# Hash attention with feed-forward: loads of batch 0 regrouped, head halves kept in the first four steps, and the whole order remade

## The chip, the cores and the metric

The kernel runs on one core of a Trainium2 chip. The metric is device time in microseconds (us), lower is better. Each kernel was executed several times; one execution was also recorded by the profiler. The profile gives a span (first to last instruction, 1.7 us less than the device time in the two profiled executions of before) and the mean clock that the throttle granted to TensorE, where 1 is full speed and the records show only full and half. An execution is called slow here when it is more than 1.5% above the fastest of the same kernel, else fast. Means below are of fast runs unless the text says otherwise.

The engines are named as in the profile: PE is TensorE, PEld its weight loads, DVE is VectorE, ACT is ScalarE, POOL is GpSimd, SP is SyncE. SPq, ACTq and POOL `DMA_DIRECT2D` lines are issues of transfers.

## The reference

Inputs q, k, v have shape (4, 8, 768, 64), `proj` is (64, 6), the feed-forward weights are 512x2048 and 2048x512.

```python
q_bits = (einsum('bhsd,dk->bhsk', q, proj) > 0)     # 6 hash bits per row
k_bits = (einsum('bhsd,dk->bhsk', k, proj) > 0)
mask   = (bucket of q == bucket of k)               # all six bits agree
scores = where(mask, q @ k.T / 8, -1e9)
x      = softmax(scores) @ v                        # heads joined to (4, 768, 512)
xn     = (x - mean) / sqrt(var + 1e-6) * g_ln
out    = x + relu(xn @ w_ch1) @ w_ch2
```

## The kernel before

The whole schedule is one string of words, `operation.engine.arguments`. A loop reads the string once and emits the instructions. Each engine then executes its own words strictly in that order, and waits where the data of a word is not there yet.

```python
with tc.manual_schedule():
    for word in ORDER.split():
        name, eng, *args = word.split(".")
        OPS[name](ENGINES[eng], *map(int, args))     # v DVE, a ACT, p POOL, s SP, t PE
```

A step s (0 to 71) stands for 256 query rows (u = s//6), a group of four heads (g) and a block of 256 keys (kp = s%3). The words that matter here:

```python
def lx(eng, g, t, kp):                 # batch 0: load a third of q (t=0) or k (t=1), 256 KB
    src = qk_view(t, 0, g).rearrange("p (c kp x) -> p kp c x", c=CC, kp=3)
    dst = Xt(0, g, t).rearrange("p (c kp x) -> p kp c x", c=CC, kp=3)
    eng.dma_start(out=dst[:, kp], in_=src[:, kp])

def tn(eng, g, t, kp):                 # transpose that third, on DVE
    for j in range(2):
        turn(tp(g, t, kp), Xt(0, g, t), j, 2 * kp, 2)

def ca(eng, g, t, kp):                 # cast it to bf16, on any of three engines
    cast(eng, t, qk(t, 0, g)[:, :, 256 * kp : 256 * kp + 256], tp(g, t, kp))

# ha: hash matmul on PE.  bi: its sign as "bits", on DVE, into G.
# lv: a v load of 32 partitions.  cv/su/sp/sc: cast of v, and its sum over the rows.

def lw1(eng, n):                       # a quarter of the first weights, cast by the DMA
    nc.gpsimd.dma_start(out=w1_sb[:, :, 512*n : 512*n+512], in_=w1ap[:, :, 512*n : 512*n+512])

def heads(h):                          # h = 0, 1: a half of the heads; h = 2: all four
    return slice(0, 4) if h == 2 else slice(2 * h, 2 * h + 2)

def S_(eng, s, h):                     # scores on PE: the bits G (6 rows), then q and k (32 rows)
    for kk in range(2):
        for rep in range(3):
            for i in range(4)[heads(h)]:
                ...                    # one matmul, 256 columns
def E_(eng, s, h):                     # exponential on ACT
    nc.scalar.activation(E(s)[:, heads(h)], sc(s, h), AF.Exp, scale=EXP_SCALE, bias=bias_sb)
# A: attention times v on PE.  na nb nc ce: division, layer norm on DVE.
# F R D: feed-forward 1, relu, feed-forward 2.  Z: residual.  O: output store.
# LX tu CA hm bt mo: loads, transposes, casts and hashes of batches 1 to 3.
```

There are three buffers for E, one score PSUM tile per half of the heads, and four buffers for X.

The softmax here doesn't subtract the row's maximum and nothing guards it: scores larger than these inputs give would overflow.

## Time and profile before

| | before |
|---|---|
| device time, median of 3 | 319.82 us (319.4 to 319.95) |
| profiled execution (a slow one) | 326.67 us, span 325.0, clock 0.957 |
| PE busy | 310.7 us (96%) |
| half-clock stretch | 24.3 to 51.6 us |

The first fence has lines of the profile page: busy time of PE, then PE's busy tenths and granted clock in 40 slices of 8.1 us.

```profile
PE 310.7 (96%) x4320; PEld 211.8 (65%) x4320; DVE 182.9 (56%) x356; ACT 182.0 (56%) x198; POOL 91.5 (28%) x102
...
PE   6869999999989999999999999999999999999993
...
PEclk9995558999999999999999999999999999999999
```

From the fourth slice on TensorE is nearly always busy, so time is lost only where the clock digit drops or where TensorE stands. Most of both lies in the first 60 us. The table by stretches shows it; the columns are the stretch, its length, then busy time (and count) of PE, PEld, DVE, ACT and POOL, granted clock, DMA share and GB/s.

```profile
20.00:25.00 5.00, 2.45 (x35) 1.69 (x31) 2.71 (x8) 2.12 (x2) 2.38 (x5) 0.93 1.12 235
25.00:40.00 15.00, 15.00 (x150) 9.89 (x151) 8.80 (x18) 6.58 (x6) 10.79 (x14) 0.50 0.91 201
40.00:50.00 10.00, 9.85 (x115) 7.00 (x108) 6.68 (x16) 6.65 (x7) 2.30 (x3) 0.50 1.24 205
```

TensorE works half of 20 to 25 us, then runs at half speed to the end of these lines. What stood before the gap is in the timeline of DVE; the bracket gives the idle time before the instruction and what ended it.

```profile
22.03 2.07 DVE L244 STREAM_TRANSPOSE tp<-X 128x256 f32<-128x256 f32 x6 [3.43 <-DMA X<-in_q_dram]
```

DVE stood 3.43 us for a piece of q that is used only some steps later, and held up all of its later words. The chain of work that ended last (start, duration, what) has the same transfer, and later two loads of v for batch 1:

```profile
4.92 5.60 DMA X<-in_k_dram
10.53 11.40 DMA X<-in_q_dram
...
72.04 6.15 DMA vn<-in_v_dram
...
80.26 2.12 DMA vn<-in_v_dram
```

This profile fell on a slow execution.

### The profile page before, as it was taken

Reading aid. Unit: us, or ns where it says so; the run is one execution under the profiler, and the core shown is the slowest. Engines: PE = TensorE matmul, PEld = TensorE weight load, DVE = VectorE, ACT = ScalarE, POOL = GpSimd, SP = SyncE. Lnnn points to the kernel's source line nnn. Section 1 sums busy time; section 2 is a strip of 40 time slices with the busy share of each in tenths; the row PEclk is TensorE's granted clock in tenths of the full one; section 3 lists DMA queues with packets and bytes.
Section 4 is the critical chain, followed back from the end, with each engine's and each line's share of the span. In section 5 each row is a group of like instructions: output and inputs, shape, how many; then the busy total and the mean of one; then the engine's idle time right before and its main releaser. Section 6 shows DMA issues by size and latency. Waiting matters only on the chain.

```text
span 325.0 us, 9793 instructions
## 1 busy us (share of the span) xinstructions
PE 310.7 (96%) x4320; PEld 211.8 (65%) x4320; DVE 182.9 (56%) x356; ACT 182.0 (56%) x198; POOL 91.5 (28%) x102
## 2 busy tenths in 40 slices
PE   6869999999989999999999999999999999999993
PEld 6555767766656767657677667666667666766651
DVE  4547475716645958765825628914635546446441
ACT  3553476666456676646756656764776675771000
POOL 2065822603470054474220056700300100001000
PEclk9995558999999999999999999999999999999999
DMA  7999799146117981463154140111220400402122
GB/s 198 216 219 275 130 205 162 23 133 165 51 38 272 302 189 57 144 173 119 22 146 86 32 117 0 39 25 23 53 53 2 114 20 2 99 2 48 50 67 65
DMA packets 33354, 33.59 MB, mean 103 GB/s; under 512 B 15648, under 2 KB 29984, under 8 KB 33312
## 3 DMA queue, kind: packets, MB, share of 16 engines
q1 hardware_dynamic: 29008, 28.77, 34.9%
q0 software_dynamic: 4224, 4.19, 8.0%
q8 instruction: 34, 0.56, 0.8%
q14 instruction: 8, 0.07, 0.1%
q10 hardware_dynamic: 80, 0.00, 0.0%
HBM read 27.53 MB, written 6.29 MB: 104 GB/s over the span
## 4 chain that ended last, share of the span: by engine, by line
PE 78%; DMA 8%; DVE 6%; SPq 4%; POOL 2%; issue 1%; ACT 0%; DVEq 0%; ACTq 0%
PE f L477 24%; PE f L492 23%; PE sc L405 17%; PE acc L420 11%; DMA X<-in_q_dram 4%; DMA vn<-in_v_dram 3%; SPq L382 2%; PE hp L370 2%; DVE xc L450 2%; DMA X<-in_k_dram 2%; PE hf L306 2%; SPq L292 1%; DVE st L446 1%; DVE x L442 1%; DVE y L433 1%
## 5 line engine op out<-in xcount | busy, mean ns | idle before, releaser
L411 ACT ACTIVATE E<-sc,bias_sb 128x1024 bf16<-128x1024 f32 x144 | 153.7, 1111 | 82.2 <-PE sc L405 80.3
L477 PE MATMUL f<-xnT,w_sb 128*128 128x256 bf16 x768 | 99.2, 273 | 0.5 <-DVE hb L487 0.5
L492 PE MATMUL f<-w_sb,hb 128*128 128x512 bf16 x384 | 93.6, 379 | 0.0
L477 PEld LDWEIGHTS <-w_sb 128*128 128x128 bf16 x768 | 70.8, 98 | 23.4 <-issue 9.9
L487 DVE TENSOR_SCALAR hb<-f 128x512 bf16<-128x512 f32 x53 | 36.6, 691 | 63.8 <-PE f L477 63.5
L405 PE MATMUL sc<-qb,kb 32*128 32x256 bf16 x1152 | 62.9, 281 | 0.0
L492 PEld LDWEIGHTS <-hb 128*128 128x128 bf16 x384 | 35.6, 98 | 35.4 <-issue 3.8
L405 PE MATMUL sc<-G 6*128 6x256 bf16 x576 | 48.6, 285 | 0.4 <-ACT E L411 0.2
L420 PEld LDWEIGHTS <-E 128*128 128x128 bf16 x1152 | 43.3, 100 | 8.0 <-issue 5.1
L420 PE MATMUL acc<-vaug,E 128*128 128x65 bf16 x1152 | 46.9, 198 | 0.2 <-POOL vaug L328 0.2
L405 PEld LDWEIGHTS <-kb 32*128 32x128 bf16 x1152 | 35.5, 98 | 3.2
L485 ACT ACTIVATE hb<-f 128x512 bf16<-128x512 f32 x43 | 25.6, 596 | 20.6 <-PE f L477 20.5
L455 POOL TENSOR_SCALAR rs<-mv 128x2 f32<-128x2 f32 x12 | 8.5, 710 | 98.1 <-DVE mv L449 97.8
L497 DVE SCALAR_TENSOR_TENSOR res<-f,rs,x 128x512 f32<-128x512 f32 x24 | 17.9, 745 | 28.3 <-PE f L492 21.6
L405 PEld LDWEIGHTS <-G 6*128 6x128 bf16 x576 | 17.3, 94 | 22.4 <-issue 19.5
L244 DVE STREAM_TRANSPOSE T<-X 128x384 f32<-128x384 f32 x48 | 24.9, 553 | 3.6 <-DMA X<-in_k_dram 3.4
L336 POOL TENSOR_TENSOR t<-vn 128x768 f32<-128x768 f32 x8 | 15.2, 1905 | 34.6 <-DMA vn<-in_v_dram 20.2
L328 POOL CAST vaug<-vn 128x768 bf16<-128x768 f32 x16 | 13.9, 889 | 39.0 <-DMA vn<-in_v_dram 30.3
L433 DVE SCALAR_TENSOR_TENSOR y<-vsB,acc 128x520 f32<-128x520 f32 x24 | 16.5, 689 | 9.0 <-PE acc L420 8.7
L450 DVE SCALAR_TENSOR_TENSOR xc<-x,mv,gB 128x512 bf16<-128x512 f32 x24 | 19.9, 829 | 0.9
L306 PE MATMUL hf<-tp,pfull 128*128 128x256 f32 x48 | 15.1, 447 | 5.2 <-DVE tp L244 4.2
L442 DVE TENSOR_TENSOR x<-y,rc 128x512 f32<-128x512 f32 x24 | 18.4, 767 | 0.8
(49 smaller groups left out, 153.1 us busy)
## 6 DMA issues: line engine op xcount, KB each, us to landing
vn<-in_v_dram SPq DMA_DIRECT2D x32, 192.0 KB
out_dram<-res SPq DMA_DIRECT2D x44, 128.0 KB
X<-in_q_dram SPq DMA_DIRECT2D x6, 768.0 KB
X<-in_k_dram SPq DMA_DIRECT2D x6, 768.0 KB
w_sb<-in_moe_w_ch_dram POOLq DMA_DIRECT2D x8, 512.0 KB, 11.1
X<-in_k_dram SPq DMA_DIRECT2D x6, 256.0 KB
X<-in_q_dram SPq DMA_DIRECT2D x6, 256.0 KB
G<-B SPq DMA_DIRECT2D x96, 4.5 KB
```

The costliest lines, as they stand in the source:

```text
L244: nc.vector.transpose(d[:, j], s[:, j, kj0 : kj0 + n])
L306: nc.tensor.matmul(hf(g, t, kp)[:, :256], pfull[:, j], tp(g, t, kp)[:, j], start=(j == 0), stop=(j == 1))
L405: nc.tensor.matmul(sc(s, i // 2)[:, i % 2, 256 * kk : 256 * kk + 256], lh, rh, start=(rep == 0), stop=(rep == 2), skip_group_check=True,)
L411: nc.scalar.activation(E(s)[:, heads(h)], sc(s, h), AF.Exp, scale=EXP_SCALE, bias=bias_sb)
L420: nc.tensor.matmul(acc[:, qt, (D + 1) * i : (D + 1) * (i + 1)], E(s)[:, i, 256 * kk + P * qt : 256 * kk + P * qt + P], vaug(u // 3)[:, 4 * ...
L433: nc.vector.scalar_tensor_tensor(yt(u, g), vs, EPS_ROW, made[f"acc{u}{g}"][:, :, :A], op0=AOP.mult, op1=AOP.add,)
L442: nc.vector.tensor_tensor(xo, a[:, :, :, 0:D], rc.to_broadcast([P, 2, 4, D]), op=AOP.mult)
L450: nc.vector.scalar_tensor_tensor(xc(u)[:, t], xt(u)[:, t], mv(u)[:, t, 0:1], gB, op0=AOP.subtract, op1=AOP.mult,)
L477: nc.tensor.matmul(f1[:, n].rearrange("p (t x) -> p t x", t=2), w1_sb[:, dt, P * nt : P * nt + P], xnT(u)[:, :, dt], start=(dt == 0), stop ...
L485: nc.scalar.activation(hb(u)[:, 2 * p : 2 * p + 2], f1, AF.Relu)
L487: eng.tensor_scalar_max(hb(u)[:, 2 * p : 2 * p + 2], f1, 0.0)
L492: nc.tensor.matmul(f2, hb(u)[:, nt, P * t : P * t + P], w2_sb[:, nt], start=(nt == 0), stop=(nt == NNT - 1),)
```

## The change

The intent is to load batch 0 with fewer, larger transfers on two hardware queues, to have the weights early, to avoid the cost of head halves as soon as the start is over, and to lay the order out anew around that.

```diff
-    def lx(eng, g, t, kp):
-        src = qk_view(t, 0, g).rearrange("p (c kp x) -> p kp c x", c=CC, kp=3)
-        dst = Xt(0, g, t).rearrange("p (c kp x) -> p kp c x", c=CC, kp=3)
-        eng.dma_start(out=dst[:, kp], in_=src[:, kp])
+    def lx(eng, g, t, kp0, kp1):
+        src = qk_view(t, 0, g).rearrange("p (c kp x) -> p c kp x", c=CC, kp=3)
+        dst = Xt(0, g, t).rearrange("p (c kp x) -> p c kp x", c=CC, kp=3)
+        eng.dma_start(out=dst[:, :, kp0:kp1], in_=src[:, :, kp0:kp1])
```

The rest is the order string. "..." marks cuts:

```diff
  loads of batch 0, in the order of their queues
- SP:   lx.s.0.1.1 lx.s.0.0.0 lx.s.0.1.0 lx.s.1.0.0 lx.s.0.0.1 lx.s.0.1.2 lx.s.1.1.1 lx.s.1.1.0
-       lv.s.0.0.0 lv.s.0.0.1 lv.s.0.0.2 lv.s.0.0.3 lx.s.1.1.2 lv.s.0.4.3 lx.s.1.0.1 lv.s.0.4.0 ...
- POOL: lw1.p.2 after three attention steps (25 us), .1 .0 .3 later
+ SP:   lx.s.0.0.0.1 lx.s.0.1.0.1 lx.s.0.1.1.3 lx.s.1.1.0.3 lv.s.0.4.1 lv.s.0.0.3 lv.s.0.0.2
+       lx.s.0.0.1.3 lg.s lv.s.0.4.0 LX.s.1.0.0 LX.s.1.0.1 ...
+ ACT:  lv.a.0.4.2 lv.a.0.0.0 lx.a.1.0.0.1 lv.a.0.0.1 lv.a.0.4.3 lx.a.1.0.1.3
+ POOL: lw1.p.2 lw1.p.1 lw1.p.3 (10 to 13 us), lw1.p.0 (20 us)
  DVE after the first attention steps
- ... lv.s.0.4.1 tn.v.1.0.1 tn.v.0.0.1 ha.t.0.0.1 A.t.1.0 tn.v.1.1.2 ca.p.1.1.2 ...
+ ... A.t.0.0 lx.s.0.0.1.3 tn.v.0.0.2 bi.v.1.0.0 S.t.4.2 E.a.4.1 E.a.4.0 A.t.1.0 bi.v.1.1.0 ...
  steps 4 to 9: whole heads instead of halves
- S.t.4.0 E.a.4.0 S.t.4.1 E.a.4.1 ... S.t.9.0 ... S.t.9.1
+ S.t.4.2 E.a.4.1 E.a.4.0 ... S.t.9.2 E.a.9.1 E.a.9.0
  last outputs
- Z.v.11.1 O.s.11.1.1 O.s.11.1.0 O.s.11.1.2 O.s.11.1.3
+ Z.v.11.1 O.s.11.1.1 O.a.11.1.2 O.a.11.1.3 O.s.11.1.0
```

`lx.a.1.0.1.3`, for example, is the load of blocks 1 and 2 of q of head group 1 on ACT's queue. Batch 1's loads of q, k and v are issued much earlier too.

## The prediction

> **What bounds the kernel now.** TensorE is busy 310.7 of 325.0 us (engine table), and 199.5 of the 200 us from 100 to 300 (table by stretches). So the time is TensorE's work, plus its idle or slow time in the first 100 us, plus the tail. The granted clock is 0.50 from 24.3 to 51.6 us with TensorE fully busy: 27.3 x 0.5 = 13.6 us lost, so work at full clock is about 297 us. The profiled run (326.7 us) is slow against the timed ones (319.8), which probably lose less clock and wait more.
>
> Before 100 us:
> - Batch 0 loads go through SyncE at about 0.63 us an issue. 512 B packets alone move 280-300 KB/us (not slow); from 10 us, with v pieces (32 partitions each) among them, 180-210.
> - VectorE stands 3.43 us, to 22.03, before a q piece needed only steps later: a wait imposed by order. TensorE stands 2.4 us behind it; then the clock halves. The Trainium skill ("TensorE: Matmul & The Clock Gate", Part 1) says that low matmul activity halves the clock; the trace agrees in place, and full clock returns just when 128-row feed-forward matmuls start (51.7).
> - At 72-83 us the chain of waits runs over batch 1's v loads (6.15 and 2.12 us), issued between small G copies; TensorE idles 2.0 us between 75 and 100.
> - Tail: last result at 320.75, end at 325.0, four output issues in a row.
>
> **What the change does.** Bytes are the same; 12 q/k transfers become 7. Larger packets gain little in rate. Six loads on ScalarE's queue save SyncE issue time only (the skill's "DMA: Bandwidth & Descriptors", "Issuing engines are not separate DMA queues", says the same); in exchange ScalarE issues before its qb cast. First score matmul unchanged: 8.3-9.5 us (8.74 before).
> Three of four w1 loads move from 25 us on to about 10 us, each about 2.6 us of the whole DMA (200 KB/us written when alone), against v. First attention-times-v matmul later: 19-22 us against 18.4.
> The false wait at 22 us goes: those transposes now stand where data has come.
> Whole-head scores in steps 4-9: 0.77 us a step against 1.08 for two halves (timeline, full clock): 6 x 0.31 = 1.9 us less work, but the exponentials need 2.2 us a step, so part only becomes idle time.
> Feed-forward starts after 9 steps, not 10, its weights already there: about 34-42 us against 51.7, so the half-clock stretch shrinks or goes. Batch 1's v loads are issued before the transposes and G copies: the stall at 72-83 goes (2 us). Last outputs on two queues: 1 us.
>
> **Sum.** -1 to -2 (heads), -1 to -2 (batch 1), -1 (tail), 0 to -3 (false wait, clock), +1 to +2 (weights against v): about -4.5 us.
>
> Predicted 315.3 us, range 309 to 320.5. Faster by over 2%: 0.33; within 2%: 0.61; slower: 0.06.
>
> **What would show it.** Right: no DVE wait over 2 us on q near 22 us; first feed-forward matmul before 43 us; fewer half-clock microseconds; no v wait in the chain at 72-83; end within 3.5 us of the last result; 100-300 us full as before. Wrong: first attention-times-v matmul after 23 us with TensorE idle before it.
>
> **What would make it wrong.** Weights starving v longer, and a clock throttled longer by it (slower); timed runs of before that carry the half clock which the change removes (then 306-310); new in-order waits in the remade order.

## The result, and the profile after

| | before | after |
|---|---|---|
| device time, median of 4 | 319.88 us (319.4 to 320.76) | 328.98 us (327.99 to 333.99) |
| ratio of fast runs | | 1.0271 (95%: 1.0225 to 1.0317): slower |
| profiled execution | slow: span 325.0, clock 0.957 | fast: span 326.2, clock 0.966 |

A ratio here is the mean time of one kernel's fast runs over that of the other's of the same rounds, so it is not quite the ratio of the medians in the table.

The change cost 2.7%. A split by clock helps. Span times mean granted clock estimates the time that the run would have taken at full clock, and the rest of the span what half clock cost; it is an estimate, because it takes TensorE to be the limit all through the half-clock stretches. Over 27 fast executions of before, in all the sets, the mean span is 318.7 us: 312.1 at full clock and 6.6 lost to half clock. Three fast executions of after have 326.8: 316.4 and 10.5. So of the 8.1 us, about 4.2 are more idle time or work, and about 3.9 are more half clock. Single executions scatter: the full-clock part goes from 308.4 to 314.2 us in before and from 315.1 to 318.5 in after.

The same lines of the profile page of after (43 of PE's 4320 matmul records are missing here, all from the second feed-forward matmul, so its busy time is under-counted after 60 us):

```profile
PE 302.0 (93%) x4277; PEld 208.4 (64%) x4320; DVE 186.7 (57%) x361; ACT 179.4 (55%) x195; POOL 88.6 (27%) x100
...
PEclk9995679799999999999999999999999999999998
```

The fair thing to compare with is a fast execution of before, that of c0_before:

```profile
PE 303.9 (95%) x4320; PEld 208.4 (65%) x4320; DVE 181.1 (57%) x356; ACT 181.8 (57%) x198; POOL 90.6 (28%) x102
...
PEclk9999769999999999999999999999999999999999
```

The digits dip to 7 and 6 in c0_before, and to 5, 6, 7 and 7 in after. The half-clock stretches add up to 10.2 us in c0_before (35.6 to 45.8), and to 20.5 us in after: 24.2 to 37.9, then 3.4 us each from 44.7 and from 61.8 (1.6 us at the very end of after are left out). The table by stretches, first of c0_before:

```profile
20.00:25.00 5.00, 3.62 (x65) 2.71 (x63) 2.87 (x9) 2.41 (x3) 3.55 (x5) 1.00 1.12 226
25.00:40.00 15.00, 13.59 (x205) 9.50 (x201) 11.97 (x30) 9.88 (x10) 10.58 (x15) 0.85 1.09 236
...
60.00:65.00 5.00, 5.00 (x72) 3.00 (x63) 0.00 (x0) 2.76 (x3) 0.00 (x0) 1.00 0.27 73
```

and of after:

```profile
20.00:25.00 5.00, 1.05 (x28) 0.90 (x31) 1.30 (x4) 0.98 (x1) 4.03 (x5) 0.92 1.16 285
25.00:40.00 15.00, 15.00 (x171) 9.61 (x164) 8.46 (x17) 6.46 (x6) 5.59 (x6) 0.57 1.14 289
...
60.00:65.00 5.00, 3.34 (x33) 2.09 (x30) 4.88 (x9) 1.96 (x2) 4.41 (x3) 0.68 0.54 220
```

From 20 to 25 us TensorE does 1.05 us of work, against 3.62. From 25 to 40 us it is "always busy", yet at clock 0.57 it finishes 171 matmuls where c0_before finishes 205 in 13.59 us of busy time. The share of busy time does not tell this; the count and the clock do.

The timeline of after shows what TensorE stood for. These are lines of several engines, in order of time:

```profile
9.78 1.76 POOL L313 DMA_DIRECT2D w_sb<-in_moe_w_ch_dram  x2
...
11.79 0.55 SPq L290 DMA_DIRECT2D X<-in_q_dram  x1
...
12.77 0.74 POOL L313 DMA_DIRECT2D w_sb<-in_moe_w_ch_dram  x1
...
18.27 0.55 ACTq L290 DMA_DIRECT2D X<-in_q_dram  x1
...
23.70 0.77 DVE L242 STREAM_TRANSPOSE tp<-X 128x256 f32<-128x256 f32 x2 [5.15 <-DMA X<-in_q_dram]
24.40 0.72 DVE L245 TENSOR_SCALAR G<-hf 128x256 bf16<-128x256 f32 x2
24.84 0.40 PE L403 MATMUL sc<-G 6*128 6x256 bf16 x4 [3.82 <-DVE G L245]
```

Read from the bottom: the scores of step 4 stood 3.82 us for the bits that DVE computes at 24.40. Their hash had been ready, but DVE's previous word, `tn.v.0.0.2`, stood 5.15 us for its data. The data is a q load that was issued at 11.79 and landed at 23.70, behind and among three weight loads issued at 9.8 to 12.8. The irony is that the block transposed there is first used in step 13 of the order. In the fast execution of before the wait at this time, for another piece of q, is short:

```profile
21.76 2.08 DVE L241 STREAM_TRANSPOSE tp<-X 128x256 f32<-128x256 f32 x6 [1.85 <-DMA X<-in_q_dram]
```

What the DMA moved from 10 to 24 us shows what the q load shared the engines with. The lines are queue, packets, MB, and the time of its packets as a share of the stretch for 16 engines; q0 is GpSimd's queue (the weights), q10 is ACT's and q1 SyncE's. First after, then m1 (an experiment below, with the weight loads later and one more q load on SyncE):

```profile
q0 software_dynamic: 1004, 1.00, 42.8%
q10 hardware_dynamic: 1233, 1.18, 40.9%
q1 hardware_dynamic: 903, 1.10, 30.8%
```

```profile
q1 hardware_dynamic: 1630, 2.32, 70.6%
q10 hardware_dynamic: 1104, 1.05, 39.4%
```

In all, 3.30 MB were moved in after and 3.39 in m1. While the weights moved their 1.00 MB, SyncE's queue, which has the late q load, moved 1.10 MB in place of 2.32 (about 0.5 of these are the q load moved there).

The chain that ended last, of after, has the same transfer and one more item that before does not have:

```profile
2.88 8.89 DMA X<-in_k_dram
11.79 11.89 DMA X<-in_q_dram
...
58.59 3.06 DVE qb L251
```

That item is the cast `ca.v.0.0.2`, which takes 0.43 us when DVE does it at 18.12 us on another block. The timeline around it:

```profile
57.24 4.12 POOL L251 TENSOR_SCALAR qb<-T 128x1536 bf16<-128x1536 f32 x1 [5.78 <-DVE T L242]
...
58.50 3.14 DVE L251 TENSOR_SCALAR qb<-tp 128x512 bf16<-128x512 f32 x1
...
61.69 0.58 PE L403 MATMUL sc<-qb,kb 32*128 32x256 bf16 x8 [1.66 <-DVE qb L251]
```

GpSimd began a cast at 57.24 that lasted to 61.36. DVE's cast ended 0.28 us after that, and TensorE stood 1.66 us for it, with 3.4 us of half clock behind. (The half clock does not follow such a hole each time: the profile of h1_after_start has the same hole of 1.66 us, to 58.53, and no half clock after 29.7 us until the tail.) The Trainium skill, "SBUF — State Buffer", section "Who interferes with whom", says that DVE's two-port operations and GpSimd take a shared pair of ports for a whole instruction, that the later one "fully blocks", and that ACT waits for neither. The trace agrees with that reading, by the 3.06 against 0.43 us and by the moment of the end.

The new order also has two holes of TensorE much later, which before and c0_before do not have (none over 0.7 us after 100 us there). In the timeline of after:

```profile
112.30 1.03 PE L475 MATMUL f<-xnT,w_sb 128*128 128x256 bf16 x8 [1.37 <-ACT E L409]
...
188.90 1.46 PE L490 MATMUL f<-w_sb,hb 128*128 128x512 bf16 x6 [0.95 <-DVE res L495]
```

The second is an in-order wait: the residual `Z.v.4.1`, which frees the PSUM tile, stands behind layer-norm words on DVE. The first is put down to an exponential that the code does not make that matmul depend on, so it stays unexplained.

### The profile page after: what moved, and what is told of

The parts are those of the page before. It is cut to its first block, busy times and chain, and to the rows that moved or that the text cites. A ratio compares the mean times of both kernels' runs of the same rounds, so it can differ in the third digit from the quotient of the medians.

```text
span 326.2 us, 9751 instructions
## 1 busy us (share of the span) xinstructions
PE 302.0 (93%) x4277; PEld 208.4 (64%) x4320; DVE 186.7 (57%) x361; ACT 179.4 (55%) x195; POOL 88.6 (27%) x100
## 4 chain that ended last, share of the span: by engine, by line
PE 78%; DVE 9%; DMA 9%; issue 1%; SPq 1%; ACT 0%; DVEq 0%
PE f L475 25%; PE f L490 22%; PE sc L403 16%; PE acc L418 10%; DMA X<-in_q_dram 4%; DMA X<-in_k_dram 3%; PE hp L368 3%; PE hf L304 2%; DMA xnT<-xc 2%; DVE xc L448 2%; DVE st L444 1%; DVE x L440 1%; DVE qb L251 1%; DVE res L495 1%; DVE y L431 1%
## 5 line engine op out<-in xcount | busy, mean ns | idle before, releaser
L475 PE MATMUL f<-xnT,w_sb 128*128 128x256 bf16 x768 | 100.3, 275 | 2.4 <-ACT E L409 1.4
L490 PE MATMUL f<-w_sb,hb 128*128 128x512 bf16 x341 | 85.9, 380 | 4.1 <-issue 1.0
L485 DVE TENSOR_SCALAR hb<-f 128x512 bf16<-128x512 f32 x55 | 37.9, 689 | 68.0 <-PE f L475 65.3
L403 PE MATMUL sc<-qb,kb 32*128 32x256 bf16 x1152 | 57.4, 277 | 1.7 <-DVE qb L251 1.7
L403 PE MATMUL sc<-G 6*128 6x256 bf16 x576 | 44.7, 281 | 5.4 <-DVE G L245 3.8
L418 PE MATMUL acc<-vaug,E 128*128 128x65 bf16 x1152 | 45.6, 195 | 1.1 <-POOL vaug L326 1.1
L403 PEld LDWEIGHTS <-kb 32*128 32x128 bf16 x1152 | 32.6, 96 | 4.2 <-issue 1.8
L483 ACT ACTIVATE hb<-f 128x512 bf16<-128x512 f32 x41 | 24.4, 595 | 18.0 <-PE f L475 18.0
L448 DVE SCALAR_TENSOR_TENSOR xc<-x,mv,gB 128x512 bf16<-128x512 f32 x24 | 18.8, 785 | 0.8
L251 POOL TENSOR_SCALAR qb<-T 128x1536 bf16<-128x1536 f32 x4 | 16.4, 4108 | 10.4 <-DVE T L242 10.4
```

Of the source, the lines that this page charges most:

```text
L403: nc.tensor.matmul(sc(s, i // 2)[:, i % 2, 256 * kk : 256 * kk + 256], lh, rh, start=(rep == 0), stop=(rep == 2), skip_group_check=True,)
L418: nc.tensor.matmul(acc[:, qt, (D + 1) * i : (D + 1) * (i + 1)], E(s)[:, i, 256 * kk + P * qt : 256 * kk + P * qt + P], vaug(u // 3)[:, 4 * ...
L448: nc.vector.scalar_tensor_tensor(xc(u)[:, t], xt(u)[:, t], mv(u)[:, t, 0:1], gB, op0=AOP.subtract, op1=AOP.mult,)
L475: nc.tensor.matmul(f1[:, n].rearrange("p (t x) -> p t x", t=2), w1_sb[:, dt, P * nt : P * nt + P], xnT(u)[:, :, dt], start=(dt == 0), stop ...
L483: nc.scalar.activation(hb(u)[:, 2 * p : 2 * p + 2], f1, AF.Relu)
L485: eng.tensor_scalar_max(hb(u)[:, 2 * p : 2 * p + 2], f1, 0.0)
```

## The experiments

Two theories stood at first. One: early weight loads and early batch 1 loads hold back the pieces of q, and TensorE pays. Two: the word `tn.v.0.0.2` stands too early on DVE, whatever the loads do. Rivals that came later: the whole-head scores of steps 4 to 9 end the turn-taking of PE and ACT (H in the expectations); the loss comes later in the order; the blocked cast. Each set of kernels ran on one chip with its own runs of before. Edits are given as words of the order, against after unless said otherwise.

### c0_before: the kernel before, unchanged

No edit.

> The kernel before, unchanged: a control, and a profile that should fall in the fast state (the one at hand, 326.7 us, did not). Both theories: ratio 1.00 within 0.5%; the profiled span should be about 318 us with a mean granted clock above 0.98, against 0.957 in the slow profile. If the fast profile also has a long half-clock stretch, then the changed kernel's half-clock stretches (20.5 us in its profile) explain less of its loss than I think.

Measured: median 321.59 us, ratio 1.0035 (0.9982 to 1.0087), profiled span 318.8 at clock 0.984. It has 10.2 us of half clock from 35.6 to 45.8, where the profile that the prediction used had 27.3 us. DVE's wait is 1.85 us instead of 3.43. So the base of the prediction was a slow execution with more to gain than the timed ones.

### e1_weights_late, e2_transpose_late, e3_both: one suspect at a time, then both

```diff
  e1: three weight loads behind the casts of v
-  lw1.p.2 lw1.p.1 lw1.p.3                      (before and within steps 0 to 2)
+  cv.p.0.0.2 lw1.p.2 lw1.p.1 lw1.p.3
  e2: the transpose just before batch 1's loads
-  lx.s.0.0.1.3 tn.v.0.0.2 bi.v.1.0.0
+  ca.v.0.0.1 tn.v.0.0.2 LX.s.1.0.0
  e3: both
```

> The changed kernel with its three early w1 loads issued only after the casts of v (about 20 us instead of 10). Theory W (the early weights hold up the q and v pieces of batch 0): the q transpose that lands at 23.7 us lands 3 to 5 us earlier, the vector engine's wait of 5.15 us shrinks below 2 us, and 4 to 8 us of the 9 us loss come back (ratio to before 1.00 to 1.015). Theory O (the order on the vector engine makes a wait of any late piece): under 3 us come back, because the piece is still far back in its queue (ratio 1.018 to 1.03).

> The changed kernel with one transpose (third q block of group 0, first used some 12 steps later) moved behind the bit tests and casts that steps 3 to 5 need; loads unchanged. Theory O: TensorE's hole at 20 to 25 us (1.05 us busy of 5) closes by 3 us or more and 4 to 8 us come back (ratio 1.00 to 1.015). Theory W: the v pieces and other q pieces are as late as before, so the wait moves to the next load and under 3 us come back (ratio 1.018 to 1.03).

> Both edits. If the start of the kernel is the whole loss (W and O are parts of one cause): 7 us or more come back, ratio 0.985 to 1.005. Rival R (the loss sits in the remade order after 60 us, the 3 us vector cast at 58.6 us and the wait for the transposes at 92 us): ratio stays above 1.015 whatever the start does.

Measured: e1 1.0236 (1.0153 to 1.0319), from two fast runs; e2 1.0399 (1.0307 to 1.0492); e3 gave only one fast run of four (median 329.75 us, 324.8 to 330.1), so it has no ratio. None brought the time back. In e2 and e3 the wait did not vanish; it moved. (The only trace of e1 is of an execution at half rate, told of below. DVE does not wait for q there, but all its words come later, so this trace settles nothing.) The timeline of DVE in e2:

```profile
36.97 0.77 DVE L240 STREAM_TRANSPOSE tp<-X 128x256 f32<-128x256 f32 x2 [5.53 <-DMA X<-in_q_dram]
```

With the early stand gone, DVE stands 5.53 us for the next piece of q, the one whose load is the last on ACT's queue, and TensorE idles from 35.58 to 38.93. In e3 the profile (a slow run) shows a hole from 24.96 to 27.55, because four weight issues of about 0.8 us each now stood on GpSimd before the sums of v, and then a DVE wait of 4.36 us to 32.82 for the same piece of q. So neither theory is right as a single cause: e2 and e3 show a row of waits behind each other, and taking away the first shows the next.

One thing remains unexplained: the profiled execution of e1 took 587.93 us, with TensorE at half rate all along (feed-forward matmuls of 439 ns on average against 275) while the trace has no clock event and reads 1.0. It happened in this one execution; the other three took 327.39, 332.98 and 328.96 us.

### h1_after_start, h2_before_start: which half of the order holds the loss

```diff
  h1: after up to D.t.0.0.0 (about 60 us), then the words of before that remain
  h2: before up to F.t.0.0, then the words of after that remain
```

> Start of the kernel before (its loads, half heads and order up to about 50 us, 40 us of TensorE work), followed by the changed kernel's order for all that is left. If the loss sits in the start (theory S: loads and order of the first 50 us), most of the 8 to 9 us is gone: 318 to 323 us, ratio 0.995 to 1.008. If it sits in the remade rest (rival R): 325 us or more, ratio above 1.015.

> The converse: start of the changed kernel (grouped loads on both queues, early weights, whole heads in steps 4 to 9, up to about 65 us), then the order of the kernel before. Theory S: still 325 to 330 us, ratio 1.015 to 1.03. Rival R: 318 to 322 us, ratio below 1.008.

Measured: h2 1.0575 (1.0525 to 1.0624), with holes of 4.07 and 7.95 us at the seam, to 59.92 and 71.44. The seam was badly chosen, so h2 tests nothing. h1 gave 1.0086 (1.0029 to 1.0144): it still has the hole before step 4 (3.55 us) and the one before step 13 (1.66 us), yet it loses a third of what after loses. This rests on two fast runs; of its two slow ones, one (327.99 us) is only 0.06 us over the line, and with it h1 would be 1.3% above before. By the split, the two fast runs have a mean of 314.7 us at full clock and 7.4 lost to half clock, against 312.1 and 6.6 in before and 316.4 and 10.5 in after. So the start costs about 2.6 us at full clock and the rest of the order another 1.7. This is a rough estimate: the two runs have 316.9 and 312.4 us, so the difference between them is larger than either number. The two later holes (1.37 and 0.95 us) are of the size of the 1.7 us and are not there in h1. That they are its cause is read from the traces and was not tested.

### e4_batch1_late: batch 1's early loads put off

```diff
-  LX.s.1.0.0 LX.s.1.0.1 lv.s.1.*    (within steps 3 to 5, and at the start of the feed-forward)
+  E.a.5.0 LX.a.1.0.0 LX.a.1.0.1 ... LX.s.1.1.0 lv.s.1.*
```

> The changed kernel with the q, k and v loads of batch 1 (3 MB, first used after 50 us) issued later: q and k of one group by ScalarE after the exponentials of step 5, v after the first load of the second group. Weights and order of batch 0 unchanged. Theory C (loads that are needed late crowd those needed now): the q piece that landed at 23.7 us lands before 21, the vector engine's 5.15 us wait falls below 2.5 us, and 3 to 7 us come back (ratio 1.005 to 1.018). If nothing but the order of instructions matters, or the weights alone crowd: under 2 us come back (ratio 1.02 to 1.03).

Measured: 1.0262 (1.0218 to 1.0307). DVE still stands 3.85 us, to 25.40. Batch 1's loads alone are not the cause.

### e5_holes: the cast moved to ACT, and step 7 earlier

```diff
-  ca.v.0.0.2
+  ca.a.0.0.2
-  ft.t.0.0 ce.v.0.1 rs.p.0 ft.t.0.1 fc.v.0.1 S.t.7.2 E.a.7.1 E.a.7.0
+  S.t.7.2 E.a.7.1 E.a.7.0 ft.t.0.0 ce.v.0.1 rs.p.0 ft.t.0.1 fc.v.0.1
```

> The changed kernel with two later holes of TensorE filled: step 7's scores and exponentials stand before the transposes of the first tile (which wait for the vector engine's normalisation until 44.9 us), and the cast of the third q block, 3.06 us on the vector engine while GpSimd makes a 4.1 us cast, goes to ScalarE. If each hole costs its idle time (2.3 and 1.7 us) and a short half-clock stretch after it (3.4 us at half rate, 1.7 us each): 4 to 7 us come back (ratio 1.005 to 1.016). If such holes are only refilled later: under 2 us (ratio 1.02 to 1.03).

Measured: 1.0281 (1.0232 to 1.0331). The hole before step 13 is gone, as expected, but a new one of 1.67 us stands before step 7, and the one before step 4 (2.59 us) stays. The second half of the edit was a bad idea, and so this run does not measure the cast.

### f4_halves, f5_before_whole: are the head halves the cause?

Halves let ACT start on the first half of a step while TensorE works on the second. f4 brings the halves back in after for steps 4 to 9; f5 does the reverse in before.

```diff
  f4, after:    S.t.4.2 -> S.t.4.1 S.t.4.0, and so for steps 5 to 9
  f5, before:   S.t.4.0 ... S.t.4.1 -> S.t.4.2, and so for steps 5 to 9 (some E words move with them)
```

> The changed kernel with the scores of steps 4 to 9 in two head halves again (six words split in two, nothing else). Theory H (turn-taking: whole-head scores write both score buffers, so they wait for both exponentials of the step before, and ScalarE then waits for them; before the feed-forward begins nothing else fills the time): the exponentials of steps 4 to 9 come closer together by about 0.8 to 1.2 us a step, the feed-forward begins 3 to 6 us earlier, and 3 to 7 us come back in spite of 1.9 us more TensorE work (ratio 1.005 to 1.018). Rival L (late loads alone set the pace of the start): no gain or a small loss from the added work (ratio 1.022 to 1.035).

> The converse, one part of the change alone: the kernel before with whole-head scores in steps 4 to 9, loads unchanged. Theory H: slower than before by 3 to 7 us (ratio 1.01 to 1.022), with ScalarE waiting 0.8 to 1.2 us before each exponential pair in those steps. Rival L: 1 to 2 us faster, for the saved TensorE work (ratio 0.993 to 1.0).

Measured: f4 1.0309 (1.0272 to 1.0346), f5 0.9986 (0.9945 to 1.0028). Halves do not help after, and whole heads do no harm in before that these runs can tell. This rival falls. A term of the prediction's sum is not confirmed either: 1 to 2 us were expected from whole heads, and f5 shows 0.14%, which is 0.4 us. Its interval goes from a gain of 1.8 us to a loss of 0.9, so it includes zero and does not rule out a gain of 1 us.

### f1_loads_undone: the old loads in the new order

```diff
-  7 lx (5 on SP, 2 on ACT), 4 lv on ACT
+  12 lx and 8 lv on SP, in about the order of before; the rest of after as it is
```

> The changed kernel with batch 0's loads as before: 12 pieces of q and k and the v pieces, all from SyncE in about the old order; weights, batch 1's loads, whole heads and instruction order as changed. Rival L (the grouped loads bring the pieces in the wrong order): the waits of the vector engine on q pieces near 23 us go below 2 us and 3 to 7 us come back (ratio 1.005 to 1.018). Theory H alone: under 2 us come back (ratio 1.02 to 1.03). If both hold, each of this and the half-head run gives back a part.

Measured: 1.058 (1.0518 to 1.0642), twice the loss. The timeline of DVE:

```profile
34.57 0.77 DVE L241 STREAM_TRANSPOSE tp<-X 128x256 f32<-128x256 f32 x2 [11.63 <-DMA X<-in_q_dram]
```

`tn.v.0.0.2` stands 11.63 us here, as its block is nearly the last in the old loads, and TensorE idles 9.24 us before step 4. Taking the large transfers and the second queue away does not help by itself, then: it is the pair of a load order and an engine order that has to fit. This is the clearest run on what one word in the wrong place costs on an in-order engine.

### g1_before_tail: two small parts of the change, in before

```diff
-  O.s.11.0.0 O.s.11.0.3 O.s.11.1.0 O.s.11.1.3
+  O.a.11.0.0 O.a.11.0.3 O.a.11.1.0 O.a.11.1.3
-  tn.v.1.0.1                                  (at its place)
+  bi.v.1.1.0 tn.v.1.0.1
```

> A candidate: the kernel before with only the last four output issues split over two queues and one early transpose moved behind the bit test that it held up. All theories: 0.8 to 2 us faster than before (ratio 0.994 to 0.998), as the tail after the last result shrinks from 5.0 to 4.2 us as it did in the changed kernel.

Measured: 0.9987 (0.9942 to 1.0033). Nothing that these runs can tell from zero. (The edits are like those of the change, not the same word for word.) In the profile the last result is ready 3.7 us before the end, against 4.2 in c0_before.

### k1 to k4: all suspects removed, and each put back alone

k1_all has five edits in after; k2, k3 and k4 each put one of them back.

```diff
  1 weights:    lw1.p.0 lw1.p.2 after su.p.0.0, lw1.p.3 lw1.p.1 after cv.p.0.4.0   (k2: early again)
  2 q load:     lx.a.1.0.1.3 -> lx.s.1.0.1.3, right after lx.s.0.0.1.3
  3 cast:       ca.v.0.0.2 -> ca.a.0.0.2
  4 batch 1:    as in e4                                                          (k3: early again)
  5 transpose:  tn.v.0.0.2 after ca.v.0.0.1                                       (k4: early again)
```

> The changed kernel with five edits together: w1 loads after the first v sums, batch 1's loads later, the early transpose of the third q block later, the second q load of group 1 on SyncE directly behind that of group 0 instead of on ScalarE after step 2's exponentials, and the slow 3 us vector cast on ScalarE. Theory M (several waits side by side, each of them enough to hold TensorE): hole before step 4 under 1.5 us, and 6 us or more come back (ratio at or below 1.008, perhaps below 1 for the 1.9 us of saved work and the shorter tail). Rival: the loss is not in these waits, ratio stays above 1.018.

> The same, but the w1 loads early as in the changed kernel. If the early weights bind: 3 us or more slower than the run with all five edits; if not, within 1.5 us of it.

> The same five edits, but batch 1's loads early as in the changed kernel. If these crowd the start: 3 us or more slower than the run with all five; if not, within 1.5 us of it (or faster, as they then stand ready).

> The same five edits, but the third q block's transpose early in the vector engine's order as in the changed kernel. If in-order waiting binds even with its piece landing early: 2 us or more slower than the run with all five; if the landing was the whole matter: within 1.5 us.

Measured:

| kernel | ratio, 95% | mean span, fast runs |
|---|---|---|
| k1_all | 1.0152 (1.0095 to 1.0209) | 322.9 |
| k2_weights_early | 1.0170 (1.0106 to 1.0235) | 323.6 |
| k3_batch1_early | 1.0103 (1.0041 to 1.0165) | 321.0 |
| k4_transpose_early | 1.0087 (1.0031 to 1.0144) | 320.7 |

The five together bring back nearly half of the loss. (One of the runs of before in this set took 317.48 us, so that four others at about 323 us count as slow; if these counted, all four ratios would be about 0.004 lower.) Batch 1's early loads and the early transpose are not harmful once the other three edits are in: the means with them are even lower, though the intervals overlap. So two of the first suspects can be left as they are, and the next kernel does that. Early weights do show in the trace of k2: TensorE stands 3.00 us, to 34.62, for a cast of v and 1.56 us, to 37.99, for a sum of v. The trace of k1 has neither wait.

### m1_weights_q_cast, m2_cast_only: three edits, and one of the three

```diff
  m1, in after
-  lw1.p.2 lw1.p.1 lw1.p.3 lw1.p.0             (at their places)
+  su.p.0.0 lw1.p.0 lw1.p.2 ... cv.p.0.4.0 lw1.p.3 lw1.p.1
-  lx.a.1.0.1.3
+  lx.s.0.0.1.3 lx.s.1.0.1.3
-  ca.v.0.0.2
+  ca.a.0.0.2
  m2, in after: the last of the three alone
```

> The changed kernel with three edits: w1 loads after the first v sums, second q load of group 1 on SyncE behind that of group 0, the blocked cast on ScalarE. If these three carry the gain: 321 to 323.5 us, ratio 1.004 to 1.012, as with the runs that had four or five edits (mean ratios 1.009 to 1.015). If the early transpose or batch 1's early loads also bind once both are back: 325 us or more.

> The changed kernel with only the cast of the third q block moved from the vector engine (3.06 us while GpSimd runs its 4.12 us cast) to ScalarE. If the hole before step 13 (1.66 us) and the half-clock stretch after it (3.4 us at half rate, 1.7 us) are really lost time: 2 to 4 us back, ratio 1.013 to 1.021. If later work absorbs them: under 1 us back, ratio 1.023 to 1.03.

Measured: m1 1.0072 (0.9989 to 1.0155), by three fast runs of 319.51, 322.57 and 320.39 us; its three slow ones took 324.64, 328.32 and 328.57. m2 1.018 (1.0119 to 1.0241), median 326.9 us. The mean span of fast runs is 319.0 us in m1 (311.7 at full clock, 7.2 lost), 324.1 in m2 (314.3 and 9.7), and 318.7 in before.

Here is the timeline of DVE in m1, at the word that stood 5.15 us in after:

```profile
19.28 0.77 DVE L240 STREAM_TRANSPOSE tp<-X 128x256 f32<-128x256 f32 x2
```

There is no bracket: the data was there. The table by stretches of m1 has TensorE busy all through 20 to 25 us, though at clock 0.78, and at clock 0.89 from 25 to 40:

```profile
20.00:25.00 5.00, 5.00 (x72) 3.87 (x72) 1.16 (x5) 2.66 (x4) 4.84 (x6) 0.78 1.05 272
25.00:40.00 15.00, 11.36 (x202) 8.33 (x202) 11.26 (x28) 9.12 (x9) 9.80 (x12) 0.89 1.18 253
```

In m2 the two waits for q are still there:

```profile
25.98 0.77 DVE L240 STREAM_TRANSPOSE tp<-X 128x256 f32<-128x256 f32 x2 [3.81 <-DMA X<-in_q_dram]
...
38.22 0.77 DVE L240 STREAM_TRANSPOSE tp<-X 128x256 f32<-128x256 f32 x2 [3.22 <-DMA X<-in_q_dram]
```

Together they settle most of the cause. The place of the weight loads and of one q load, with the cast on ACT, bring the mean of the fast runs back to within 1% of before, with an interval from a gain of 0.1% to a loss of 1.6%. With the cast on ACT the hole before step 13 is gone in m2 as it was in e5. The cast alone gives part of the time (1.018 against 1.0271 of after, measured in different sets, with intervals that overlap). m1 and m2 ran in one set and differ by the other two edits alone, the weights and the q load. Their fast runs do not overlap (319.5 to 322.6 us against 324.8 to 327.2), so the pair is worth about 5 us by the means of fast runs, 4 by those of all runs. The two were only put together in after as a pair; which of them does more is open. k2 hints that the weights matter less, since putting them early again cost k1 only 0.2%, within the intervals; but that was in the company of edits 4 and 5.

### What was not reached

No kernel clearly beats both. f5_before_whole (0.9986) and g1_before_tail (0.9987) are not told apart from before. m1 still has the first of the two later holes (1.62 us, to 103.52), although it does less work on TensorE than before does by its whole heads. It also has the larger share of slow runs: over all six its mean is 324.0 us, against 321.5 for the eleven runs of before in the same set, 0.8% more. A version of m1 without the two later holes was not run.

## Why the prediction was wrong

The prediction was 315.3 us with a range of 309 to 320.5, most likely within 2%. The result was 328.98 us, slower by 2.7% by the ratio: outside the range, and in the direction that was given a chance of 0.06.

The step that failed is this one: "The false wait at 22 us goes: those transposes now stand where data has come." The three transposes that DVE made together at 22 us in before do stand so in after: they run at 14.68, 31.00 and 32.67 us without a wait. But the remade order puts another one, `tn.v.0.0.2`, in front of the words that step 4 needs, and the prediction did not set the landing of its load against its place. So the wait did not go but got longer: 5.15 us, to 23.70, in after, against 1.85 us in a fast execution of before and 3.43 in the slow one, and TensorE stood 3.82 us behind it, with 13.65 us of half clock from 24.2 us on. f1_loads_undone (11.63 us) and m1 (no wait) show that this wait is set by the pair of load order and word order.

Point by point:

- **Weights against v, "+1 to +2".** Mis-sized, and aimed at the wrong tensor. v did come in time: the first attention times v began at 20.13 us (19 to 22 predicted). It was q that came late, in 11.89 us from issue to landing, and q stood on an in-order engine in front of words that TensorE needed. With the q wait gone, k2 shows the wait for v too, 3.00 us, but at 34.62. h1 puts the cost of the start roughly at 2.6 us at full clock.
- **False wait and clock, "0 to -3".** The sign was wrong. "Fewer half-clock microseconds" was false against a fast execution of before (10.2 us became 20.5), though true against the slow one (27.3). By the mean of fast runs half clock cost 3.9 us more.
- **Feed-forward before 43 us.** False. The timeline has the first of these matmuls at 47.70 in after and at 46.00 in c0_before; m1, with its weights *later*, begins at 40.99. Having the weights early was not what the start of the feed-forward hung on.

Those three lines, of after, c0_before and m1 in that order:

```profile
47.70 2.12 PE L475 MATMUL f<-xnT,w_sb 128*128 128x256 bf16 x16
```

```profile
46.00 2.86 PE L474 MATMUL f<-xnT,w_sb 128*128 128x256 bf16 x24
```

```profile
40.99 1.91 PE L473 MATMUL f<-xnT,w_sb 128*128 128x256 bf16 x16
```

- **Whole heads, "-1 to -2".** Not confirmed. f5 measures 0.4 us with an interval from a gain of 1.8 us to a loss of 0.9. The prediction itself said that part would become idle time; how much did was not measured.
- **Batch 1, "-1 to -2".** The mechanism was right: no v load is in the chain from 72 to 83 us of after. But from 65 to 100 us TensorE was busy 33.69 us against 33.01 in c0_before, so it gave about 0.7 us, not 2 (somewhat more if some of the missing records fall into this stretch).
- **Tail, "-1".** Right in the traces, though no timed run shows it: g1, with a like edit, is not told apart from before. The last result was ready at 322.83 us of a span of 326.2, which leaves 3.4 us, against 313.85 + 0.75 = 314.60 of 318.8, 4.2 us, in c0_before. The timeline of DVE, c0_before first:

```profile
313.85 0.75 DVE L494 SCALAR_TENSOR_TENSOR res<-f,rs,x 128x512 f32<-128x512 f32 x1 [2.65 <-PE f L489]
```

```profile
322.08 0.75 DVE L495 SCALAR_TENSOR_TENSOR res<-f,rs,x 128x512 f32<-128x512 f32 x1 [2.65 <-PE f L490]
```

- **Larger transfers and two queues: little.** No run tests this alone. The Trainium skill, "DMA: Bandwidth & Descriptors", section "Issuing engines are not separate DMA queues", says that starting transfers from several engines saves only the time of issuing. The trace is in line with that: with three queues loading at once, one q load took 11.89 us to land, and the load on ACT's queue, issued at 18.27, moved its last packet at 31.41.
- **First score matmul 8.3 to 9.5 us.** Right: 9.48.
- **100 to 300 us full as before.** Not quite: the two later holes lie there.
- **Not foreseen at all.** The cast that stood behind GpSimd (1.66 us of idle time, then 3.4 us of half clock), and the two later holes (2.3 us together). "New in-order waits in the remade order" was named as what would make the prediction wrong, and it is what happened; a slower result was given a chance of only 0.06.

The four terms of gain summed to 3 to 8 us. What the traces and runs show in their place is gains of about 0.7 us (batch 1) and 0.8 us (tail) and none that can be told from zero for whole heads. Against that stand net losses of about 2.6 us at the start by h1, about 1.7 us later in the order, and 3.9 us of half clock. The terms are from different executions and are rough.

How certain each part is: that the place of the weight loads, the q load and the cast together make up most of the loss is shown by m1; that the first two as a pair carry about 5 us of it, by m1 against m2. That halves, batch 1's loads or the early transpose alone do is ruled out by f4 and f5, e4 and k3, e2 and k4. The share of the later holes is only read from traces. The clock is in part chance: the time lost to half clock goes from 2.8 to 9.9 us over the fast executions of before.

## What to carry to other kernels

On engines that work in order, a word whose data comes late costs every word behind it, so check each early word of a remade schedule against the landing time of its load, and put words that are needed only much later after those that TensorE waits for. When a wait is taken away and the time does not move, look for the next wait behind it: here single edits at the start gave no gain that could be told from noise, and three edits together gave most of it. Take the base of a prediction from a profile in the same state as the timed runs, and compare counts and clock, not only busy shares.

## What the Trainium skill lacked or had wrong

- "TensorE: Matmul & The Clock Gate", Part 1, has the clock go to half after an idle window of about 3.4 us and back to full after one busy window of that length. The length fits: the half stretches are 3.4, 10.2 and 13.65 us, near multiples of 3.41. The first part fits only roughly and only once: half clock came at 24.2 us in after, 3.2 us into the 3.82 us hole. But it came at 35.6 us in c0_before and at 44.7 in after, with no hole over 0.81 us in the 5 us before, and in the slow profile of before after a hole of 2.42 us. The second part does not fit: the clock stayed at half for 13.65 us (27.3 in the slow profile of before) while the profile shows TensorE busy nearly throughout. In after, 6.1 us of that work is hash matmuls on 128 rows, in fp32; nearly all the rest is score matmuls on 6 or 32 rows and attention matmuls of 65 columns. The page says nothing of how long such work keeps the clock down.
- The same page warns that clock events in traces are unreliable and tells of a clock stuck low for over 50 us. It has nothing on a whole execution at half rate: e1 took 587.93 us once, with mean clock 1.0 on record and feed-forward matmuls of 439 ns instead of 275.
- The same page says that the slow matmuls at the start of a kernel vary from run to run, but no page gives the spread of the mean clock of whole executions of one program. The executions of before had mean clocks of 0.949 to 0.991, and spans of 315.8 to 325.0 us.
- "DMA: Bandwidth & Descriptors" has no figure for how long one load takes when three queues share the engines: a q load took 11.89 us from issue to landing here, with the DMA share above 1.1.
